# Loading and converting the first three weight pieces ahead of the loop, in a one-core kernel of attention and two MoE layers

## The chip, the cores and the metric

The kernel runs on one core of a Trainium2 chip. The metric is the device time of one execution in microseconds (us), lower is better; three runs of the kernel before are given by their median.

## What is computed

The reference, cut to what matters: an attention that keeps the 32 largest scores of each row, a dense gated MLP ("the first MoE") and a mixture of eight experts with one expert a token ("the second MoE").

```python
# q, k, v: 4 x 8 heads x 576 x 64
scores = scale * np.matmul(q, k.transpose(0, 1, 3, 2))
kth = np.partition(scores, -32, axis=-1)[..., -32:-31]
scores = np.where(scores >= kth, scores, -1e9)
attn = np.exp(scores - scores.max(-1, keepdims=True))
attn = attn / (attn.sum(-1, keepdims=True) + 1e-9)
x = np.matmul(attn, v)                    # 2304 tokens x 512
# first MoE: w_in 512 x 2048, w_out 2048 x 512
h = x @ w_in
x = (h * np.clip(h + 3.0, 0.0, 6.0) / 6.0) @ w_out
# second MoE: 8 experts, 512 -> 1024 -> 512
logits = x @ w_gate
e = argmax(logits); out = softmax(logits)[e] * (relu(x @ w1[e]) @ w2[e])
```

The inputs to the first MoE's weights arrive in 64-bit words, which is why its weights need a conversion.

## The kernel before

**Tiles and stages.** The work of the attention is cut into 144 tiles of 128 query rows of one head (or two heads' tails). Heads go in pairs; a *visit* is a pair of heads with up to 256 of its query rows, four tiles as a rule. Tiles 0 to 3 belong to the first pair, 4 to 7 to the second, and so on. For a pair the kernel loads the keys (tiles `kd` for 512 of them, `ke` for the tail of 64), splits them on POOL (for the first pair on ACT and DVE) into a high and a low part (`kprep`, L434 on), transposes them on PE into `misc` (one buffer, L449 and L457) and copies them to `kx` on ACT (L452, L462). Queries follow in `qprep` (L468 on): loaded to `qn`, transposed (L474), copied to a high part `qh` on ACT (L482), the low part `ql` made on DVE (L492).

For a tile, `qk` writes scores to PSUM (`sps`, four matmuls of L630, two for each half of the keys), `sevac` copies them to an SBUF tile `sbuf` on ACT (L300), `top_a` searches them on DVE: eight MAX8 of 72 columns each (L660, `cd`) and rounds of MAX8 and MATCH_REPLACE (L666, L671, `m` and `cw`). ACT scales the maximum and a threshold (`nb`, `uall`), takes the exponential (L712) and counts signs (L721). For the first 20 tiles a z step finds the exact threshold: POOL writes a mask z (L703, 2.2 us), PE adds it to the scores in `yps` (six matmuls of L630, the first with `identb` as weights; `z_pe`), DVE searches the sum (L731) and masks the exponentials (L735, L739). Then PE transposes them and multiplies with the values (L755, L789).

**The weights of the first MoE.** `conv64` (L309 on) converts one piece of 128 x 512 elements, alternately of `w_in` (i0, i1, ...) and `w_out` (o0, o1, ...), 32 pieces in all. It is a generator with a load step and four more: the load of 512 KB into a `raw` buffer (L316, three buffers); on ACT a square (L328, into `sq`, which is the only buffer of the tag `jk` that also serves the signs of the tiles) and a sign with a sum (L333), on DVE a shift (L329); two more DVE steps (L336, L339); on POOL the copy of the high part (L298) and the subtraction that makes the low one (L347). `conv_load` keeps three pieces loading, `conv_next` takes the front one through its steps and loads another. The loop over tiles takes one piece in nearly every step, `cacc` adding `CRATE` = 15 sixteenths of one. MoE step g forces the pieces that it needs.

**What sets the order.** The program is written tile by tile; a scheduler then orders the instructions of each engine by a priority (`pr`, from a table `PRIO`, lowest first, plus `STEP` = 400 for each step) and its own estimates. After that each engine works strictly in its order, and so does each queue of loads; nearly all loads go through that of the SyncE (SP). A priority can have a lower bound, its second argument. A write of one element into a tile by POOL ahead of its load (L315, from `ts[0]["s"]`, the scores of tile 0) holds the first three piece loads back: they can't start until POOL has read that tile.

The head of the loop before, in which `ensure(t)` prepares the keys and queries that tile t needs:

```python
        loads(0)
        boot.extend([yps[0], yps[1], None, l1ps])
        for t in range(LA):
            ensure(t)
            qk(t)
            sevac(t)
            if t == 0:
                conv_load()
```

Of the kernel before, what the change touches and what calls it, by code (L numbers as in the profile page):

```python
# [13 lines left out]
F32 = mybir.dt.float32  # L14
# [36 lines left out]
    load=-1940, epi_a=370, top_c=55, exp=-295, need=75, qk=10, pv=-40, sevac=390, xevac=440, trans=210, xt0=75,  # L51
# [6 lines left out]
def attention_two_moe_kernel(  # L58
# [13 lines left out]
    PE, V, A, G, SP = nc.tensor, nc.vector, nc.scalar, nc.gpsimd, nc.sync  # L72
# [75 lines left out]
    def r_(ap):  # L148
        return ap.bitcast(F32)
# [4 lines left out]
    def pr(name, least=0):  # L154
        tc.cur_priority = max(least, pr0[0] + PRIO[name])

    def run(gen):
        for _ in gen:
            pass
# [68 lines left out]
    def body(cs, exact, ends=None):  # L228
# [67 lines left out]
        def copy(pool, dst, src):  # L296
            if pool:
                G.tensor_scalar(dst, src, 1.0, 0.0, op0=ALU.mult, op1=ALU.add)  # L298
            else:
                A.activation(dst, src, AF.Copy)  # L300
# [3 lines left out]


        csum = m1p.tile([P, 2 * NF1], F32, name="csum")
        wcnt = [0]

        def conv64(src, a_, nm, parts):  # L309
            n_ = DM // a_  # L310
            pr("load", pbase + 8 * len(wload))
            raw = m1p.tile([P, a_, n_, 2], U32, tag="ysb", bufs=NRAW, name=f"raw{nm}")
            if nm in ("i0", "o0", "i1"):

                G.tensor_copy(raw.rearrange("p a n t -> p (a n t)").bitcast(F32)[:, 0:1], ts[0]["s"][:, 0:1])  # L315
            SP.dma_start(raw.rearrange("p a n t -> p a (n t)"), src)  # L316
            yield
            lo, hi = raw[:, :, :, 0], raw[:, :, :, 1]
            wf = m1p.tile([P, DM], F32, tag="cvs", bufs=3, name=f"cv{nm}").rearrange("p (a n) -> p a n", a=a_)
            wb = wf.bitcast(U32)  # L320
            hf = hi.bitcast(F32)
            sq = ap1.tile([P, S], F32 if exact else BF16, tag="z" if exact else "jk", bufs=2 if exact else 1,
                          name=f"sq{nm}")[:, 0:DM].rearrange("p (a n) -> p a n", a=a_)
            pr("conv")
            if CSQ:
                G.tensor_tensor(sq, hf, hf, op=ALU.mult)
            else:
                A.activation(sq, hf, AF.Square)  # L328
            V.tensor_scalar(wb, hi, 3, 0x3FFFFFFF, op0=ALU.logical_shift_left, op1=ALU.bitwise_and)  # L329
            if not exact:  # L330
                i = wcnt[0]
                wcnt[0] += 1
                A.activation(sq, sq, AF.Sign, bias=cs["ntiny"], scale=1.0, accum_out=csum[:, i:i + 1])  # L333
            yield
            pr("conv")
            V.scalar_tensor_tensor(wb, hi, 0xC0000000, wb, op0=ALU.bitwise_and, op1=ALU.bitwise_or)  # L336
            yield
            pr("conv")
            V.scalar_tensor_tensor(wb, lo, 29, wb, op0=ALU.logical_shift_right, op1=ALU.bitwise_or)  # L339
            if exact:  # L340
                G.tensor_scalar(sq, sq, TINY2, None, op0=ALU.is_ge)
                G.tensor_tensor(wf, sq, wf, op=ALU.mult)
            yield
            pr("conv")
            h, l, done = parts()
            copy(CH, h, wf)
            G.tensor_tensor(l, wf, r_(h), op=ALU.subtract)  # L347
            done()
# [15 lines left out]
        wload = []  # L364

        def conv_load():
            while wsteps and len(wload) < NRAW:
                wload.append(wsteps.pop(0))
                next(wload[-1])
# [4 lines left out]
        def conv_next():  # L374
            if wload:
                yield from wload[0]
                wload.pop(0)
                cdone[0] += 1
                conv_load()
                if not exact and cdone[0] == 2 * NF1:  # L380
                    V.tensor_scalar(csum, csum, DM - 0.5, 0.0, op0=ALU.is_lt, op1=ALU.add, accum_out=flag[:, 1:2])

        def conv_upto(i):
            while cdone[0] <= i:
                run(conv_next())
# [32 lines left out]
        kraw = {}  # L418
# [172 lines left out]
        def ensure(t):  # L591
            n = tiles[t][0]
            b, p = visits[n][:2]
            while kdone[0] <= b * NPAIR + p or qdone[0] <= n:
                loads(t)
                pk[0] = "need"
                pstart(t - 1, -2 * T)
                while pjob[0] is not None:
                    pnext()
                pk[0] = "prep"  # L600
                loads(t)

        ts = {}

        def qk(t, zw=None):
            pr("qk" if zw is None else "zpe")
            n, o = tiles[t]
            b, p = visits[n][:2]
            st = qx[n]
            kt = kx[b, p]  # L610
            for half in range(2):
                dst = (sps if zw is None else yps2)[:, half, 0:HS]
                if o == "T":

                    fw = visits[n][3] // P * P
                    mm = []
                    for i in st:
                        mm.append((dst, i[:, 0, fw:fw + P], kt[0][:, half * HS:(half + 1) * HS]))
                        a_, b_ = half * HS, min((half + 1) * HS, N4)
                        mm.append((dst[:, 0:b_ - a_], i[:, 1, fw:fw + P], kt[1][:, TAIL + a_:TAIL + b_]))  # L620
                        if half:
                            mm.append((dst[:, b_ - a_:HS], i[:, 1, fw:fw + P], kt[1][:, 0:TAIL]))
                else:
                    h, j = o
                    js = slice(j * P, (j + 1) * P)
                    mm = [(dst, i[:, h, js], kt[h][:, half * HS:(half + 1) * HS]) for i in st]
                if zw is not None:
                    mm.insert(0, (dst, identb[0], zw[:, half * HS:(half + 1) * HS]))
                for i, (d_, a_, b_) in enumerate(mm):
                    PE.matmul(d_, a_, b_, start=(i == 0), stop=(i == len(mm) - 1))  # L630

        def sevac(t):
            pr("sevac")
            ssb = sbuf[t % NSB]
            copy(mod(t, SPOOL), ssb.rearrange("p (h s) -> p h s", h=2), sps[:, :, 0:HS])
            ts[t] = {"s": ssb}
# [455 lines left out]
        pbase = pr0[0] = tc.cur_priority + STEP  # L1092
        loads(0)
        boot.extend([yps[0], yps[1], None, l1ps])
        for t in range(LA):
            ensure(t)
            qk(t)
            sevac(t)
            if t == 0:
                conv_load()  # L1100
        cacc = 0
        for t in range(T + 7):
            pr0[0] = pbase + t * STEP
# [317 lines left out]
    with tc.If(todo > 0):  # L1421
# [4 lines left out]
        for e in range(NE):  # L1426
            n = nc.values_load(ctl[0:1, 2 + e:3 + e], min_val=0, max_val=NT)
# [32 lines left out]
```

## Time and profile before

| | |
|---|---|
| median of three runs | 1199.83 us |
| lowest and highest | 1197.64 and 1202.85 us |
| the profiled execution: time | 1204.39 us |
| its span, first to last instruction | 1202.5 us |
| PE busy | 1118.5 us, 93% of the span |
| DVE busy | 940.9 us, 78% |
| ACT busy | 807.6 us, 67% |
| POOL busy | 458.5 us, 38% |
| mean granted clock of PE | 0.961 of full speed |

All times of the trace belong to the one profiled execution and count from its first instruction. A share of busy time is a mean over stages with different bounds: the attention with the first MoE runs to about 930 us, the second MoE after that, and within the attention the start, the stretch with the weight conversion (33 to about 242 us) and the rest differ. An engine's idle time says what ended it; it costs something only where that engine sets the pace.

### The profile page before, as it was taken

The page shows a single profiled execution, that of the slowest core. Times are in us where ns is not written, and L with a number is a line of the kernel's source. Part 1 is how long each engine was busy: PE and PEld are TensorE (multiplying, and loading weights), DVE is VectorE, ACT ScalarE, POOL GpSimd, SP SyncE. Part 2 cuts the span into 40 slices and gives each one's busy share as a digit, 9 for nine tenths or more (in the row PEclk, how much of TensorE's full clock was granted, in tenths as well). Part 3 has the DMA queues.
Part 4 walks back from the last instruction along what each step waited for, and adds up shares of the span by engine and source line. Part 5 has one row for each costly group of instructions (what it writes and reads, how often), then busy time and mean ns, then how long its engine had stood idle before and what let it go on. Part 6 is the DMA issues. An engine that isn't in the chain of part 4 may idle for free.

```text
span 1202.5 us, 24061 instructions
## 1 busy us (share of the span) xinstructions
PE 1118.5 (93%) x7414; PEld 1003.8 (83%) x7414; DVE 940.9 (78%) x3853; ACT 807.6 (67%) x2082; POOL 458.5 (38%) x668
## 2 busy tenths in 40 slices
PE   5677688999999999999999999999999899999995
PEld 4566577778999989999988899999888799888885
DVE  5989989999999999998999899999641554545540
ACT  4777877778878788778778788777541353444441
POOL 5877646644332354433342432322344311222110
PEclk9668879999999999999999999999999899999998
DMA  3654456564553555754444554543486555455530
GB/s 76 189 179 142 143 171 221 162 174 125 157 134 113 151 134 142 177 135 135 118 122 126 133 147 125 152 133 110 127 271 163 176 187 179 161 176 185 160 121 31
DMA packets 184123, 179.24 MB, mean 149 GB/s; under 512 B 123629, under 2 KB 148509, under 8 KB 183984
## 3 DMA queue, kind: packets, MB, share of 16 engines
q1 hardware_dynamic: 178960, 167.24, 48.3%
q0 software_dynamic: 3872, 10.08, 2.6%
q8 instruction: 61, 1.00, 0.4%
q14 instruction: 78, 0.64, 0.2%
q10 hardware_dynamic: 1152, 0.28, 0.1%
HBM read 159.53 MB, written 18.61 MB: 148 GB/s over the span
## 4 chain that ended last, share of the span: by engine, by line
PE 71%; DVE 16%; issue 5%; ACT 4%; POOL 2%; DMA 2%; SPq 0%; POOLq 0%; ACTq 0%; DVEq 0%
PE l1ps L863 15%; PE yps L894 13%; PE ptps L789 9%; PE lp L1263 8%; PE ops L1286 8%; PE sps L630 6%; PE ptps L755 4%; DVE cd L660 2%; DVE pbuf L739 2%; DVE z L696 2%; DVE z L731 1%; PE ptps L935 1%; DVE m L666 1%; DVE cw L671 1%; PE misc L474 1%
## 5 line engine op out<-in xcount | busy, mean ns | idle before, releaser
L894 PE MATMUL yps<-wo,gh 128*128 128x512 f32 x544 | 206.7, 418 | 0.1
L298 POOL TENSOR_SCALAR gh<-gf 128x256 fp32r<-128x256 f32 x144 | 72.7, 505 | 345.2 <-PE yps L894 196.0
L660 DVE MAX8 cd<-sbuf 128x8 f32<-128x72 f32 x1152 | 187.9, 218 | 3.4 <-ACT sbuf L300 3.2
L863 PE MATMUL l1ps<-xh,wih 128*128 128x256 f32 x576 | 167.6, 291 | 4.7 <-DVE gf L875 3.1
L863 PE MATMUL l1ps<-xh,wil 128*128 128x256 f32 x576 | 164.0, 285 | 0.0
L863 PE MATMUL l1ps<-xl,wih 128*128 128x256 f32 x576 | 163.9, 285 | 0.0
L789 PE MATMUL ptps<-vn,pt 128*128 128x65 f32 (+1 forms) x1152 | 145.8, 281 | 0.0
L789 PEld LDWEIGHTS ptps<-vn,pt 128*128 128x128 f32 x1152 | 143.0, 201 | 0.0
L739 DVE SCALAR_TENSOR_TENSOR pbuf<-sbuf,tall,pbuf 128x576 f32<-128x576 f32 x144 | 136.8, 950 | 0.1
L883 POOL TENSOR_TENSOR gl<-gf,gh 128x256 fp32r<-128x256 f32 x144 | 125.5, 871 | 11.4
L863 PEld LDWEIGHTS l1ps<-xh,wih 128*128 128x128 f32 x576 | 110.4, 192 | 14.9 <-DVE gf L875 7.6
L1036 DVE TENSOR_TENSOR wl<-raw,wh 128x1024 fp32r<-128x1024 f32 x64 | 78.6, 1236 | 53.7 <-ACT wh L1035 51.6
L721 ACT ACTIVATE jk<-sbuf,uall 128x576 bf16<-128x576 f32 x144 | 111.6, 775 | 4.2 <-DVE j L735 0.9
L863 PEld LDWEIGHTS l1ps<-xl,wih 128*128 128x128 f32 x576 | 110.6, 192 | 4.2
L712 ACT ACTIVATE pbuf<-sbuf,nb 128x576 f32<-128x576 f32 x144 | 111.2, 775 | 4.1 <-PE ptps L757 0.9
L894 PEld LDWEIGHTS yps<-wo,gh 128*128 128x128 f32 x544 | 101.2, 190 | 14.8 <-POOL qh L486 0.3
L300 ACT ACTIVATE sbuf<-sps 128x576 f32<-128x576 f32 x144 | 92.9, 645 | 30.4 <-PE sps L630 16.5
L869 ACT ACTIVATE gf<-l1ps,three 128x256 f32<-128x256 f32 x144 | 67.9, 471 | 66.9 <-PE l1ps L863 55.7
L755 PE MATMUL ptps<-ident,pbuf 128*128 128x128 f32 x576 | 93.9, 286 | 19.7 <-DVE j L735 12.6
L894 PE MATMUL yps<-wo,gl 128*128 128x512 f32 x272 | 110.4, 406 | 0.6 <-POOL gl L883 0.6
L863 PEld LDWEIGHTS l1ps<-xh,wil 128*128 128x128 f32 x576 | 110.6, 192 | 0.1
L630 PE MATMUL sps<-kx,qh 128*128 128x288 f32 (+2 forms) x336 | 96.8, 319 | 14.3 <-ACT sbuf L300 10.5
(259 smaller groups left out, 2974.7 us busy)
## 6 DMA issues: line engine op xcount, KB each, us to landing
wo<-wod SPq DMA_DIRECT2D x144, 512.0 KB, 3.8
raw<-in_moe_w_dram SPq DMA_DIRECT2D x64, 512.0 KB, 4.3
vn<-in_v_dram SPq DMA_DIRECT2D x96, 128.0 KB, 2.7
rawi<-in_moe_w_in_dram SPq DMA_DIRECT2D x16, 512.0 KB, 4.0
rawo<-in_moe_w_out_dram SPq DMA_DIRECT2D x16, 512.0 KB, 4.6
wod<-wc SPq DMA_DIRECT2D x16, 512.0 KB, 5.6
qn<-in_q_dram SPq DMA_DIRECT2D x126, 64.0 KB, 2.5
yd<-y SPq DMA_DIRECT2D x18, 258.0 KB, 5.1
```

The lines of the kernel that those rows point to most:

```text
L630: PE.matmul(d_, a_, b_, start=(i == 0), stop=(i == len(mm) - 1))
L660: V.max(cd[:, c, :], s[:, c * CK:(c + 1) * CK])
L712: A.activation(d["p"], d["s"], AF.Exp, bias=d["nb"], scale=SCALE)
L721: A.activation(jk, d["s"][:, 0:S], AF.Sign, bias=ts[t]["u"], scale=-1.0, accum_out=d["sg"])
L739: V.scalar_tensor_tensor(d["p"], d["s"], tall[:, t:t + 1], d["p"], op0=ALU.is_ge, op1=ALU.mult)
L755: PE.transpose(ptps[:, c * P:(c + 1) * P], pb[:, c0 + c * P:c0 + (c + 1) * P], ident)
L789: PE.matmul(d_, a_, b_, start=(i == 0), stop=(i == len(mm) - 1))
L863: PE.matmul(dst, a[:, c, fs], b_[:, c, :], start=(n == 0), stop=(n == 3 * NCC - 1))
L883: G.tensor_tensor(gl, gf, r_(gh), op=ALU.subtract)
L894: PE.matmul(acc(bk, tt), a[:, tsl], b_, start=(f == 0 and m == 0), stop=(f == NF1 - 1 and m == 2))
L1263: PE.matmul(lp, a[:, c, fs], b_[:, c, 0:w], start=(n == 0), stop=(n == 3 * NCC - 1))
L1286: PE.matmul(ops_[j][0:n], a, b_[:, ns], start=(f == 0 and i == 0), stop=(f == NF2 - 1 and i == len(ms) - 1))
```

## The change

The first three raw pieces (i0, o0, i1) are asked for ahead of the two leading tiles, their release reads an element of the first pair's loaded keys, the lower bound of their load priority is dropped, and the first two pieces are converted ahead of the loop over tiles. The conversion steps of the three take the priority `match` (560) in place of `conv` (295), and their `cv` and `sq` tiles get a release of their own, two one-element writes by POOL from the scores of tile 0 (i0, o0) or tile 1 (i1).

```diff
-        wcnt = [0]
+        wcnt = [0, 0]
...
-            pr("load", pbase + 8 * len(wload))
+            pr("load", pbase + 8 * len(wload) if wcnt[1] >= 3 else 0); wcnt[1] += 1
             raw = m1p.tile([P, a_, n_, 2], U32, tag="ysb", bufs=NRAW, name=f"raw{nm}")
             if nm in ("i0", "o0", "i1"):

-                G.tensor_copy(raw.rearrange("p a n t -> p (a n t)").bitcast(F32)[:, 0:1], ts[0]["s"][:, 0:1])
+                G.tensor_copy(raw.rearrange("p a n t -> p (a n t)").bitcast(F32)[:, 0:1], r_(kraw[0, 0][0][:, 0, 1, 1, 0:1]))
             SP.dma_start(raw.rearrange("p a n t -> p a (n t)"), src)
             yield
...
-            pr("conv")
+            early = nm in ("i0", "o0", "i1")
+            ck = "match" if early else "conv"
+            pr(ck)
+            if early:
+                G.tensor_copy(wf.rearrange("p a n -> p (a n)")[:, 0:1], ts[nm == "i1"]["s"][:, 0:1])
+                G.tensor_copy(sq.rearrange("p a n -> p (a n)")[:, 0:1], ts[nm == "i1"]["s"][:, 0:1])
...
             yield
-            pr("conv")
+            pr(ck)
             V.scalar_tensor_tensor(wb, hi, 0xC0000000, wb, op0=ALU.bitwise_and, op1=ALU.bitwise_or)
             yield
-            pr("conv")
+            pr(ck)
             V.scalar_tensor_tensor(wb, lo, 29, wb, op0=ALU.logical_shift_right, op1=ALU.bitwise_or)
...
         boot.extend([yps[0], yps[1], None, l1ps])
+        conv_load()
         for t in range(LA):
             ensure(t)
             qk(t)
             sevac(t)
-            if t == 0:
-                conv_load()
+        conv_upto(1)
```

Lines of the changed program behind L324 are numbered five higher than before (L328 is now L333, L492 is L497).

**The order on POOL at its start.** Before, the identity and the iotas follow at once; `jp` and `iota` are index tables, `ident` the identity that all transposes need:

```order
L184 IOTA jp 128x128
masks.py:199 AFFINE_SELECT ident<-ident 128x128
L189 IOTA iota_96 128x8
L192 IOTA isum 128x16
L195 IOTA tok 128x18
```

Now:

```order
L184 IOTA jp 128x128
L315 COPY rawi_187<-kd_0_176 128x1
L315 COPY rawo_190<-kd_0_176 128x1
L315 COPY rawi_193<-kd_0_176 128x1
masks.py:199 AFFINE_SELECT ident<-ident 128x128
L189 IOTA iota_96 128x8
```

The three release copies, which wait for a key load, have moved ahead of the identity and the index tables. They also stand ahead of the key split.

**The order on POOL between tile 1's scores and tile 1's z.** `vp` is a value tile, `sbuf_156` and `sbuf_157` are the scores of tiles 0 and 1, `kd_1` the second pair's keys. Before:

```order
L546 COPY vp_164<-sbuf_157 64x1 x2
L442 TENSOR_SCALAR kd_1_208<-kd_1_208 128x8x64
L443 TENSOR_TENSOR kd_1_208<-kd_1_208 128x8x64
L703 TENSOR_SCALAR z_347<-sbuf_156,uall 128x576
L703 TENSOR_SCALAR z_430<-sbuf_157,uall 128x576
L703 TENSOR_SCALAR z_498<-sbuf_158,uall 128x576
```

Now:

```order
L298 TENSOR_SCALAR wih<-cvi_246 128x4x128
L352 TENSOR_TENSOR wil<-cvi_246,wih 128x4x128
L708 TENSOR_SCALAR z_377<-sbuf_156,uall 128x576
L447 TENSOR_SCALAR kd_1_217<-kd_1_217 128x8x64
L448 TENSOR_TENSOR kd_1_217<-kd_1_217 128x8x64
L298 TENSOR_SCALAR wc_268<-cvo_259 128x512
L352 TENSOR_TENSOR wc_268<-cvo_259,wc_268 128x512
L329 CAST sqi_358<-sbuf_157 128x1
L298 TENSOR_SCALAR wih<-cvi_357 128x4x128
L447 TENSOR_SCALAR ke_1_218<-ke_1_218 64x2x64
L352 TENSOR_TENSOR wil<-cvi_357,wih 128x4x128
L448 TENSOR_TENSOR ke_1_218<-ke_1_218 64x2x64
```

Behind the last row comes tile 1's z. The six conversion instructions of the three pieces have come between, and the split of the second pair's key tail, which used to stand ahead of tile 0's scores.

**The order on PE at the second pair's queries.** `z_430` and `z_460` are tile 1's z, `misc_361` and `misc_391` receive the transposed queries. Before:

```order
L457 MATMUL misc_343<-ident,ke_1_209 128x64 x2
L630 LDWEIGHTS identb
L630 MATMUL yps<-z_430,identb 128x288
L630 MATMUL yps<-kx_0_1_188,qh_218 128x288
L630 MATMUL yps<-kx_0_1_188,ql_219 128x288
L474 MATMUL misc_361<-ident,qn_222 128x128 x4
L630 MATMUL sps<-kx_1_0_265,qh_366 128x288
```

Now:

```order
L462 MATMUL misc_373<-ident,ke_1_218 128x64 x2
L635 LDWEIGHTS identb
L635 MATMUL yps<-z_460,identb 128x288
L635 MATMUL yps<-kx_0_1_197,qh_227 128x288
L635 MATMUL yps<-kx_0_1_197,ql_228 128x288
L635 LDWEIGHTS identb
L635 MATMUL yps<-z_460,identb 128x288
L635 MATMUL yps<-kx_0_1_197,qh_227 128x288
L479 MATMUL misc_391<-ident,qn_231 128x128
L635 MATMUL yps<-kx_0_1_197,ql_228 128x288
L479 MATMUL misc_391<-ident,qn_231 128x128 x3
```

In both orders the queries stand behind tile 1's z; what has moved is that all six z matmuls now follow the key tail, and that the scores of tile 4 come after them with nothing between.

On DVE the second pair's `ql` stands after all of tile 3's search and its first round before; now it stands behind the fourth of tile 3's eight MAX8.

## Rows read from the trace of the kernel before

**Rows 1.** Stretches: length, then busy us (instructions) of PE, PEld, DVE, ACT, POOL.

```profile
12.80:33.45 20.65, 15.88 (x64) 12.37 (x64) 14.84 (x86) 12.44 (x32) 14.13 (x19) 0.92 0.47 123
33.45:60.00 26.55, 15.03 (x73) 12.95 (x72) 26.55 (x68) 20.68 (x51) 23.35 (x22) 0.68 0.64 174
60.00:180.00 120.00, 91.93 (x509) 79.60 (x509) 110.30 (x448) 94.42 (x248) 76.37 (x62) 0.77 0.52 159
...
300.00:400.00 100.00, 99.33 (x736) 92.39 (x736) 96.31 (x452) 81.24 (x230) 29.98 (x53) 1.00 0.49 136
```

**Rows 2.** Waits of DVE, 10 to 35 us; columns: total us, times, longest.

```profile
DVE z L731 <- PE yps L630: 3.9, 2, 2.9
DVE ql L492 <- ACT qh L482: 2.8, 2, 2.6
DVE cd L660 <- ACT sbuf L300: 2.5, 2, 1.9
```

**Rows 3.** Timeline, 4 to 15 us; columns: start, duration, engine, line, operation.

```profile
4.33 1.28 ACT L439 ACT_TABLE_LOAD   x1 [4.33 <-DMA kd<-in_k_dram]
...
6.28 0.69 DVE L440 TENSOR_TENSOR kd<-kd 128x512 fp32r<-128x512 f32 x1 [5.14 <-ACT kd L439]
...
7.83 0.15 DVE L210 SCALAR_TENSOR_TENSOR place<-lead,own 24x8 f32<-24x8 f32 x1
...
12.80 0.65 ACT L300 ACTIVATE sbuf<-sps 128x576 f32<-128x576 f32 x1 [0.35 <-PE sps L630]
...
13.49 1.18 DVE L660 MAX8 cd<-sbuf 128x8 f32<-128x72 f32 x8 [1.86 <-ACT sbuf L300]
```

**Rows 4.** Single lines over the span; durations in ns are min/median/max.

```profile
L329 DVE TENSOR_SCALAR cvi<-rawi x16: 400/406/1450, 33.5 to 231.2; 128x512 uint32<-128x512 uint32 x16
...
L336 DVE SCALAR_TENSOR_TENSOR cvi<-rawi,cvi x16: 665/670/678, 34.4 to 231.7; 128x512 uint32<-128x512 uint32 x16
...
L339 DVE SCALAR_TENSOR_TENSOR cvi<-rawi,cvi x16: 671/678/994, 35.2 to 232.5; 128x512 uint32<-128x512 uint32 x16
...
L347 POOL TENSOR_TENSOR wil<-cvi,wih x16: 1272/1281/1918, 38.7 to 234.1; 128x512 fp32r<-128x512 f32 x16
...
L739 DVE SCALAR_TENSOR_TENSOR pbuf<-sbuf,tall,pbuf x144: 792/810/1924, 23.5 to 863.3; 128x576 f32<-128x576 f32 x144
...
L315 POOL COPY rawi<-sbuf x2: 188/190/192, 14.1 to 14.4; 128x1 f32<-128x1 f32 x2
```

**Rows 5.** A load on the queue of SP, and loads from 0 to 60 us.

```profile
13.14 0.62 SPq L528 DMA_DIRECT2D qn<-in_q_dram  x1
...
rawi<-in_moe_w_in_dram SPq DMA_DIRECT2D x5, 512.0 KB, 4.1
```

**Rows 6.** 33.45 to 60 us: busy DVE, POOL of cvi; of cvo; two timeline rows.

```profile
33.45:60.00 26.55, 8.36 (x10) 7.14 (x6) 0.68 0.64 174
...
33.45:60.00 26.55, 8.45 (x9) 5.82 (x6) 0.68 0.64 174
...
38.67 1.57 POOL L347 TENSOR_TENSOR wil<-cvi,wih 128x512 fp32r<-128x512 f32 x1
...
39.05 1.81 DVE L739 SCALAR_TENSOR_TENSOR pbuf<-sbuf,tall,pbuf 128x576 f32<-128x576 f32 x1
```

**Rows 7.** POOL in the timeline, 16 to 23 us, and z matmuls in the chain.

```profile
16.21 0.62 POOL L442 TENSOR_SCALAR kd<-kd 128x512 fp32r<-128x512 f32 x1
...
20.81 2.21 POOL L703 TENSOR_SCALAR z<-sbuf,uall 128x576 bf16<-128x576 f32 x1 [0.30 <-ACT uall L684]
...
20.56 1.64 PE yps L630 x6
```

**Rows 8.** Timeline of the second pair's queries.

```profile
25.03 1.11 PE L474 MATMUL misc<-ident,qn 128*128 128x128 f32 x4
...
26.18 0.60 ACT L482 ACTIVATE qh<-misc 128x512 fp32r<-128x512 f32 x1 [0.94 <-PE misc L474]
...
26.81 0.69 DVE L492 TENSOR_TENSOR ql<-misc,qh 128x512 fp32r<-128x512 f32 x1 [0.21 <-ACT qh L482]
```

## The prediction

> **What bounds the kernel now.** I read the busy time by stretches first, then VectorE's (DVE's) waits in the start, then the timeline of the first 31 us. The stretches [rows 1] show the start as the one loose place: from 12.80 to 33.45 us, when the first tiles are searched, DVE works 14.84 of 20.65 us, so 5.81 are free. From 33.45 to 60 it works 26.55 of 26.55, from 60 to 180 110.30 of 120: while weights are converted, DVE sets the pace. From 300 to 400 TensorE (PE) works 99.33 of 100; there PE does. So time saved or lost on DVE in the first 40 us moves what lies behind it by about as much, while idle time of PE, ScalarE (ACT) or GpSimd (POOL) in the start costs nothing by itself.
>
> DVE's waits between 10 and 35 us [rows 2] are z of the first tiles behind PE (3.9 us in two waits, the longer 2.9), ql behind ACT (2.8 in two, the longer 2.6) and the search behind ACT's score copies (2.5 in two, the longer 1.9). The longer ql wait and the longer search wait lie before 13.49, where the search begins [rows 3].
>
> **The change, part by part.** *The three pieces.* One piece costs DVE 0.406 + 0.670 + 0.678 = 1.75 us by the medians of L329, L336 and L339 [rows 4], three of them 5.26. POOL pays 1.28 for the low half and about 0.62 for the high one (as for the key's high half, a tile of the same size) [rows 4, 7], 1.90. They leave the stretch behind 33.45 and go between the searches of tiles 0 to 2. On DVE 5.26 would fit into the 5.81 free ones. That is the whole direct gain, if nothing new is made to wait.
>
> *The release.* The three POOL copies now read a key element and wait for the keys' load, which had landed when ACT began at 4.33 [rows 3]. By the order of POOL the identity and the iotas stand behind them. At 0.19 us each [rows 4] they end by 4.9; they used to be done with long before. So DVE's small constants, which end about 7.8 as before [rows 3], now have eight of their instructions ahead of the key split: it goes from 6.28 to about 7.5, 1.2 us late. Against that, ACT now copies tile 0's scores before the second head's keys: split to 8.2, four transposes 1.1, key copy 0.6 [rows 8], four score matmuls 1.1 (six z matmuls take 1.64 [rows 7]) and the gaps between them; tile 0's copy can begin at about 11.5, where it was 12.80 [rows 3]. Tile 1 has a piece's two activations ahead of it on ACT and gains less. I take nothing for the start, with bounds -1.3 and +1.2.
>
> *The queue of SP.* The second pair's last query part went out at 13.14 [rows 5]. Two of the three piece loads and a value load, which waits for tile 1's scores, now stand ahead of it; it goes at about 16.5. A piece lands 4.1 us after its issue, also with other loads about [rows 5]. So the queries are there by about 20 and the third piece by about 18, and what wants the queries comes later still (next part). POOL's queue is the cover; were it short, the second pair would wait at 20 us for these loads.
>
> *The new wait.* This term decides. Between tile 1's score copy and tile 1's z, POOL had the key split and two z, from 16.21 on [rows 7]. Now the order of POOL gives it three conversions (3 x 1.90), two z (2 x 2.21), the key split (0.62 and, as for L347, 1.28), the key tail's (about 0.7, by its size a third of that) and a small cast (0.2): 12.9 us. From about 16.0 tile 1's z ends at 28.9, against 20.81 + 2.21 = 23.02. PE holds the second pair's query transposes behind that z: six z matmuls, 1.64, then the transposes to 31.1, qh 0.60 to 31.7, ql 0.69 to 32.4. Before, ql ended at 27.50 [rows 8]. And ql stands in the midst of tile 3's search, so DVE stops there.
>
> *DVE's account to that point.* Before, from 13.49 to 27.50, 14.01 us with 2.9 + 0.2 of waiting [rows 2, 3, 8]: 10.9 of work. Now 1.55 of it (tile 1's z search, four search steps and one round) stands behind ql: 9.35, plus 5.26 makes 14.6, from about 12.2. DVE would be through at 26.8 and is let through at 32.4. Made equal, 32.4 + 1.55 = 33.95 against 27.50 + 5.26 = 32.76: **1.2 us late**, with the pieces done.
>
> *What follows.* Before, two more waits came behind ql, 3.9 - 2.9 = 1.0 (z) and 2.5 - 1.9 = 0.6 (tile 5) [rows 2]. DVE now gets to both places late, and I leave 0.5 for tile 5: credit 1.1. Two things I can only bound. From 33.45 to 60 the 19 conversion instructions take 8.36 + 8.45 = 16.81 us [rows 6] where the medians make 10.9, a surcharge of 0.93 a piece. Three pieces fewer there save between 0, as the next ones crowd in, and 2.8. And the third pair's ql also stands behind POOL's queue: 0 to 2.3 of new waiting (tile 5's copy plus the activations ahead of that ql on ACT, less the search in between). I set the two against each other.
>
> *Contention.* L739 takes 0.810 by its median and 1.81 where it began 0.38 us after a POOL subtract [rows 4, 6]. The Trainium skill (GPSIMD Engine Reference, section 8, Key points) says that GpSimd shares its SBUF interfaces with VectorE and contends with VectorE instructions that run in a 2-port mode or have two SBUF inputs; the rows agree. By that rule the pieces would carry their surcharge, 2.8 us in all, into the start, where z and the splits keep POOL busy: it speaks against the change, and the sum would come to +2.9. By the rows most of the surcharge would fall into DVE's wait at ql, and I count none.
>
> **Sum:** 0 (start) + 1.2 - 1.1 + 0 = +0.1. The profiled execution took 1204.39 us, so 1204.5 in its frame; it lies 4.56 above the median of the runs, 1199.83. That gives 1199.9, and I say **1200.0**. The other 29 pieces come one a tile as before, on a DVE that is still the bound, so that conversion is two pieces ahead from then on gains nothing that is not in this account.
>
> **The rivals.** *Faster: the pieces lie in idle time.* If POOL's queue does not reach the second pair, for instance because the splits come sooner than I stack them, all 5.26 is hidden and some of the 2.8 goes too: -5.3 to -8.0, about 1193.5. For it: 5.81 us free. Against it: PE's order, which fixes the queries behind tile 1's z. Chance 0.17.
>
> *Slower: POOL becomes the bound of the first three pairs.* Every z passes through POOL at 2.2, behind what was queued. It decides once POOL is so far behind that DVE also stops at the z of tiles 2 and 3 and at the third pair's ql. DVE had no free time from 33.45 to 60; if it gets as much there as in the stretch ahead, 5.81, with the 1.2 of the start it is +7.0, 1206.8. For it: POOL worked 23.35 of 26.55 there already. Against it: the conversions that it did there are gone. Chance 0.13.
>
> *The change doesn't do what it says.* The copies read the element as loaded, not as split, and a piece may come late: the third is issued behind a key load that waits for PE. Price at most 1 us near 18, inside the wait at ql: 1200 again, in the forecast's chance of 0.70.
>
> **How the numbers follow.** Half a per cent, 6 us, is what a measurement of this kernel can tell from no change; its three runs spread over 5.2. The forecast lies within it: faster 0.17, same 0.70, slower 0.13. Its own range is -1.3 - 2.8 = -4.1 to +1.2 + 2.3 = +3.5, with 2 for the runs 1194 to 1205.5. To leave out no more than 2 in 10 the range goes to 1193 and 1207.
>
> **What would show it.** Right: the identity on POOL after 4.7; tile 0's copy before 12; tile 1's z ending between 27 and 30; DVE waiting 2 us or more at ql near 30; the last conversion earlier by some us, and the second MoE within 4 us of where it begins now. Wrong: ql before 28 with the pieces done (faster), or DVE idle by more than 3 us between 34 and 60 (slower). If the start is as I say and the end still moves by more than 5 us, the cause lies in a later place that I have not read.

## The result: 1.0% slower, and the profile after

The changed kernel takes 1211.80 us (median of 4 runs, 1210.13 to 1214.18), the kernel before beside it 1199.14 (4 runs): a ratio of 1.0102, 95% interval 1.008 to 1.0125. The forecast was 1200.0, no change. The profiled execution of the changed kernel took 1210.61 us, with a span of 1208.7. Lines of the changed kernel's file behind line 324 are 5 higher than before: L329 is L334, L492 is L497, L703 is L708, L739 is L744.

**The start came as forecast.** Timeline of the changed kernel (start, duration, engine, line, operation, idle time before), rows that answer to [rows 3, 5]:

```profile
4.00 0.29 POOL masks.py:199 TENSOR_SCALAR_AFFINE_SELECT ident<-ident 128x128 f32<-128x128 f32 x1
7.23 0.69 DVE L445 TENSOR_TENSOR kd<-kd 128x512 fp32r<-128x512 f32 x1
11.55 0.65 ACT L300 ACTIVATE sbuf<-sps 128x576 f32<-128x576 f32 x1 [1.30 <-PE sps L635]
12.23 0.91 DVE L665 MAX8 cd<-sbuf 128x8 f32<-128x72 f32 x6 [2.23 <-ACT sbuf L300]
16.35 0.62 SPq L533 DMA_DIRECT2D qn<-in_q_dram  x1
```

The search begins at 12.23 us, 1.3 earlier than before (13.49), and the last part of the second pair's queries is issued at 16.35, where I had about 16.5.

**Then VectorE stops twice.** Its waits from 10 to 60 us, to be held against [rows 2] (total us, times, longest; the shorter of the two ql waits, 0.98 us, is that of the first pair at 9.31):

```profile
DVE ql L497 <- ACT qh L487: 8.0, 2, 7.1
DVE z L736 <- PE yps L635: 3.4, 1, 3.4
DVE cd L665 <- ACT sbuf L300: 2.2, 1, 2.2
DVE cvi L334 <- DMA rawi<-in_moe_w_in_dram: 1.0, 1, 1.0
DVE j L740 <- ACT jk L726: 1.0, 1, 1.0
```

The stretches that answer to [rows 1] (length, then busy us and instructions of PE, PEld, DVE, ACT, POOL):

```profile
12.23:33.45 21.22, 10.87 (x39) 7.95 (x38) 14.76 (x62) 11.64 (x29) 15.92 (x24) 1.00 0.40 105
33.45:60.00 26.55, 14.61 (x70) 11.74 (x70) 20.42 (x67) 17.52 (x43) 20.99 (x20) 0.81 0.51 151
```

Two stretches tell it. Up to 33.45 VectorE does no more work than before (14.76 against 14.84 us), although three pieces were put there: it stands at ql instead of searching. From 33.45 to 60 it worked without a gap before (26.55 of 26.55) and now 20.42.

What it waits for is GpSimd's queue, and then ScalarE's and TensorE's. Timeline of the changed kernel, GpSimd from tile 1's scores to the third pair's keys, and the rows of the other engines that belong to it:

```profile
16.30 0.61 POOL L298 TENSOR_SCALAR wih<-cvi 128x512 fp32r<-128x512 f32 x1
17.00 1.47 POOL L352 TENSOR_TENSOR wil<-cvi,wih 128x512 fp32r<-128x512 f32 x1
18.57 2.28 POOL L708 TENSOR_SCALAR z<-sbuf,uall 128x576 bf16<-128x576 f32 x1
20.93 0.97 POOL L447 TENSOR_SCALAR kd<-kd 128x512 fp32r<-128x512 f32 x1
21.99 1.57 POOL L448 TENSOR_TENSOR kd<-kd 128x512 fp32r<-128x512 f32 x1
...
25.44 0.72 POOL L329 CAST sqi<-sbuf 128x1 bf16<-128x1 f32 x1
...
28.75 2.22 POOL L708 TENSOR_SCALAR z<-sbuf,uall 128x576 bf16<-128x576 f32 x1
33.54 0.60 ACT L487 ACTIVATE qh<-misc 128x512 fp32r<-128x512 f32 x1 [2.96 <-PE misc L479]
34.03 0.77 ACT L717 ACTIVATE pbuf<-sbuf,nb 128x576 f32<-128x576 f32 x1
34.16 0.69 DVE L497 TENSOR_TENSOR ql<-misc,qh 128x512 fp32r<-128x512 f32 x1 [7.05 <-ACT qh L487]
34.70 0.19 ACT L689 ACTIVATE uall<-m 128x1 f32<-128x1 f32 x1
34.98 2.21 POOL L708 TENSOR_SCALAR z<-sbuf,uall 128x576 bf16<-128x576 f32 x1 [4.01 <-ACT uall L689]
37.98 1.26 POOL L448 TENSOR_TENSOR kd<-kd 128x512 fp32r<-128x512 f32 x1
39.30 1.12 PE L454 MATMUL misc<-ident,kd 128*128 128x128 f32 x4 [1.48 <-POOL kd L448]
40.46 0.46 PE L635 MATMUL yps<-z,identb 128*128 128x288 bf16 x1
42.19 0.77 DVE L736 MAX8 z<-yps 128x8 f32<-128x576 f32 x1 [3.38 <-PE yps L635]
```

The first stop: tile 1's z begins at 28.75, with the three conversions, the key splits and tile 0's z ahead of it without a gap; behind its matmuls stand the second pair's query transposes, then qh at 33.54, then ql. The second stop follows from the first: tile 2's threshold u (L689) stands on ScalarE behind qh and the exponential, so it comes at 34.70, and GpSimd, by then idle for 4.01 us, begins tile 2's z at 34.98. Its matmuls on TensorE (40.46) stand behind the transposes of the third pair's keys (39.30), whose split GpSimd makes after that z. VectorE gets that z at 42.19. This place on TensorE is new: before, tile 2's z stood ahead of those transposes.

```profile
27.66 0.28 PE L630 MATMUL yps<-z,identb 128*128 128x288 bf16 x1 [0.43 <-POOL z L703]
29.72 1.12 PE L449 MATMUL misc<-ident,kd 128*128 128x128 f32 x4 [0.72 <-POOL kd L443]
```

In the changed kernel the z was written by 37.19, and VectorE was through with its search at 38.80. Had the six z matmuls (1.64 us [rows 7]) begun at 37.82, when TensorE had ended what it did before those transposes, they would have ended near 39.5: by this estimate a stop of 0.7 us instead of 3.38. No run changes that order alone.

**How much of the 12 us this is.** The delay is read from the start of the mask instruction (L739, now L744) of a tile, in the mean of two profiles of each kernel (the second ones are runs of the next section):

```
tile                        0      3      9     15     60    141
before, us               23.3   51.5   90.6  125.9  400.6  855.2
changed, later by us      1.3    8.3    8.4    8.0    7.8    5.8
```

All of it is there by tile 3, 60 us into the run, and behind tile 60 some 2 us of it go again. The two profiles of before are of executions near the top of its runs (1204.39 and 1206.39). Each run lists its mean granted TensorE clock: 11 executions of before at 0.960 to 0.961 have a mean span of 1201.9 us, the five of the changed kernel, with a mean clock of 0.9604, one of 1210.1. At equal clock that is 8.2 us, the delay of tile 3. All 63 executions of before that ran beside the experiments have a mean clock of 0.9645 and a mean span of 1199.7: another 2.2 us, which go with a lower clock of the changed kernel. About 2 us of the difference between the first medians are left.

### The profile page after: what moved, and what is told of

The parts are those of the page before. It is cut to its first block, busy times and chain, and to the rows that moved or that the text cites. A ratio compares the mean times of both kernels' runs of the same rounds, so it can differ in the third digit from the quotient of the medians.

```text
span 1208.7 us, 24061 instructions
## 1 busy us (share of the span) xinstructions
PE 1119.1 (93%) x7414; PEld 1005.2 (83%) x7414; DVE 943.5 (78%) x3853; ACT 807.3 (67%) x2082; POOL 454.3 (38%) x674
## 4 chain that ended last, share of the span: by engine, by line
PE 66%; DVE 17%; issue 5%; ACT 5%; DMA 3%; POOL 2%; SPq 0%; POOLq 0%; ACTq 0%; DVEq 0%
PE l1ps L868 13%; PE yps L899 11%; PE ptps L794 9%; PE lp L1268 8%; PE ops L1291 8%; PE sps L635 5%; PE ptps L760 4%; DVE cd L665 3%; DVE pbuf L744 2%; DVE z L701 2%; DVE z L736 2%; DVE m L671 1%; DVE cw L676 1%; PE ptps L940 1%; PE sps L899 1%
## 5 line engine op out<-in xcount | busy, mean ns | idle before, releaser
L744 DVE SCALAR_TENSOR_TENSOR pbuf<-sbuf,tall,pbuf 128x576 f32<-128x576 f32 x144 | 143.0, 993 | 0.1
L888 POOL TENSOR_TENSOR gl<-gf,gh 128x256 fp32r<-128x256 f32 x144 | 121.8, 846 | 11.4
L701 DVE SCALAR_TENSOR_TENSOR z<-sbuf,uall 128x576 f32<-128x576 f32 x124 | 106.8, 862 | 0.0
```

Of the source, the lines that this page charges most:

```text
L701: V.scalar_tensor_tensor(d["z"], s, d["u"], s, op0=ALU.is_le, op1=ALU.mult)
L744: V.scalar_tensor_tensor(d["p"], d["s"], tall[:, t:t + 1], d["p"], op0=ALU.is_ge, op1=ALU.mult)
L888: G.tensor_tensor(gl, gf, r_(gh), op=ALU.subtract)
```

## The experiments

Theories: **queue** (GpSimd's added work ahead of what the second and third pair need delays VectorE), **loads** (the early piece loads hold up the second pair's on the queue of SyncE), **ScalarE** (its order and added activations do), **later place** (the cost arises behind the first 60 us).

**1. The conversions behind tile 1's z.** The six GpSimd instructions are put back in the program until tile 1's threshold is there, and a one-element copy from it makes them wait:

```
+            def fin(dep=None):
...
+                h, l, done = parts()
+                if dep is not None:
+                    G.tensor_copy(h[:, 0:1, 0:1].rearrange("p a n -> p (a n)"), dep)
+                copy(CH, h, wf)
+                G.tensor_tensor(l, wf, r_(h), op=ALU.subtract)
+                done()
+            held.append(fin) if early else fin()
...
+            if t == 2:
+                while held:
+                    held.pop(0)(ts[t - 1]["m8"][:, 0:1] if exact else uall[:, t - 1:t])
```

> The changed kernel with one thing undone: the six GpSimd instructions of the three early pieces wait for tile 1's threshold and stand behind tile 1's z. Loads, VectorE's order and ScalarE's work stay those of the change. Queue theory (the GpSimd work ahead of tile 1's z made the second pair's queries late): tile 1's z ends near 24 us instead of 31.0, the first ql of the second pair runs before 29 us with under 1.5 us of idle time ahead of it instead of 7.05, and the time falls from 1211.8 to 1197-1203. Theory that the early loads get in the way on the queue of SyncE, or that ScalarE's extra activations do: ql stays near 34 and the time within 3 us of 1211.8. Theory of a later place (the starts differ by some 6 us, the medians by 12.7): the idle time goes, but the time stops at 1204-1207.

Measured: 1211.79 us, 1.0087 (1.0065 to 1.0108): a miss for the queue theory as I had put it. Timeline of that kernel:

```profile
24.62 2.21 POOL L714 TENSOR_SCALAR z<-sbuf,uall 128x576 bf16<-128x576 f32 x1 [1.86 <-ACT uall L695]
28.05 0.47 PE L468 MATMUL misc<-ident,ke 64*128 64x64 f32 x2 [2.46 <-POOL ke L454]
31.62 0.69 DVE L503 TENSOR_TENSOR ql<-misc,qh 128x512 fp32r<-128x512 f32 x1 [6.09 <-ACT qh L493]
33.54 2.21 POOL L714 TENSOR_SCALAR z<-sbuf,uall 128x576 bf16<-128x576 f32 x1
40.73 0.77 DVE L742 MAX8 z<-yps 128x8 f32<-128x576 f32 x1 [4.30 <-PE yps L641]
```

Tile 1's z is 4 us earlier than in the change, yet ql waits 6.09: TensorE first takes the transposes of the key tail, whose split now stands among the dependence copies behind z. And the three conversions now stand ahead of tile 2's z, which begins at 33.54 (25.40 before), and VectorE stops there for 4.30. The stops add up to 10.4 us, as in the change (7.05 + 3.38). GpSimd's work was moved, not taken away.

**2. The early loads alone.** One line out:

```
-        conv_upto(1)
```

> The changed kernel without the conversion of two pieces ahead of the loop over the tiles: three pieces are released and loaded as early as in the change, and converted one a tile as before, so that one conversion (1.9 us of GpSimd) stands ahead of tile 1's z instead of three. Queue theory: z of tile 1 is 1 to 2 us later than before, time 1199-1203. Theory of the loads: the second pair's queries land late as in the change, ql waits by more than 4 us, time 1207-1212.

Measured: 1200.92 us, 0.9991 (0.9981 to 1.0002), no difference from before.

```profile
22.55 2.22 POOL L708 TENSOR_SCALAR z<-sbuf,uall 128x576 bf16<-128x576 f32 x1
29.50 0.69 DVE L497 TENSOR_TENSOR ql<-misc,qh 128x512 fp32r<-128x512 f32 x1 [1.68 <-ACT qh L487]
```

The loads theory falls: same release, same queue of SyncE, and ql waits 1.68 us at most. In its profile the masks come 1.7 us earlier than before at tile 3 and 4.2 at tile 60, of which the timed runs show 1.5 us in the medians at most; that execution had a mean granted clock of 0.969, those of before 0.961 and 0.960.

**3. GpSimd's work alone, in the kernel before.**

```
+            if t == 1:
...
+                sc = ts[1]["s"][:, 0:DM].rearrange("p (a n) -> p a n", a=NCC)
+                for i_ in range(3):
+                    sl_ = slice(i_ * P, (i_ + 1) * P)
+                    G.tensor_scalar(wih[:, :, sl_], sc, 1.0, 0.0, op0=ALU.mult, op1=ALU.add)
+                    G.tensor_tensor(wil[:, :, sl_], sc, r_(wih[:, :, sl_]), op=ALU.subtract)
```

> The kernel before with three pairs of GpSimd instructions added, of the shapes of the three conversions (copy and subtract, 128 partitions by 512), reading tile 1's scores and placed ahead of the z of tiles 0 and 1; their results are overwritten later. Nothing else is changed: the loads and VectorE's and ScalarE's work are those of before. Queue theory: tile 1's z ends near 28-29 us, VectorE stops at ql for 4 us or more, and the time rises from 1199 by 5 to 8 us, to 1204-1207. Theories of the loads or of ScalarE: the time stays within 2 us of before.

Measured: 1209.43 us, 1.0066 (1.0048 to 1.0084), 7.0 us above the 1202.41 of before measured beside it.

```profile
22.32 2.22 POOL L703 TENSOR_SCALAR z<-sbuf,uall 128x576 bf16<-128x576 f32 x1
26.25 0.77 DVE L731 MAX8 z<-yps 128x8 f32<-128x576 f32 x1 [6.11 <-PE yps L630]
```

So 5.7 us of GpSimd work, with nothing else of the change, cost 7.0. VectorE stops for 6.11 us at tile 0's z instead of at ql, since five of the six instructions stand ahead of it here (the last subtract comes between the z of tiles 0 and 1). The forecast of the place was wrong; the rise of 5 to 8 us was right, though not the 1204 to 1207 that it was worked out to, since before ran at 1202.41 beside it.

**4. The kernel before again.** No edit.

> The kernel before, unchanged, for a second profile: the first one was of an execution 5 us above the median. Expected near 1199, and a span that is shorter than the first profile's in the later stages rather than in the first 60 us; if the first 60 us differ, the comparison of the two starts has to be made against this one.

One execution, 1206.39 us, span 1204.5, and not near 1199 as expected. Its masks run 1.2 us ahead of the first profile up to tile 15 and 1.2 behind from tile 70 on; between 420 and 430 us the granted clock was 0.83. The starts agree, and the comparison stands.

**5. One piece ahead of the loop instead of two.**

```
-        conv_upto(1)
+        conv_upto(0)
```

> The changed kernel with one piece converted ahead of the loop instead of two: in GpSimd's order two conversions (3.8 us) instead of three stand ahead of tile 1's z, and the second pair's key tail stands behind that z. Queue theory: tile 1's z ends 2 to 4 us earlier than in the change (27-29 us instead of 31.0), VectorE waits 3-5 us at ql instead of 7.05, and the time lies between that of the loads-only run (1200.9) and that of the change (1211.8), at 1203-1208. Theory that the chain has a step at the second piece alone: 1200-1202 or 1210-1212.

Measured: 1208.81 us, 1.0068 (1.0042 to 1.0094), 0.8 us above the range that was expected.

```profile
25.03 2.60 POOL L708 TENSOR_SCALAR z<-sbuf,uall 128x576 bf16<-128x576 f32 x1
32.09 0.69 DVE L497 TENSOR_TENSOR ql<-misc,qh 128x512 fp32r<-128x512 f32 x1 [4.59 <-ACT qh L487]
39.32 0.77 DVE L736 MAX8 z<-yps 128x8 f32<-128x576 f32 x1 [2.72 <-PE yps L635]
```

The dose is in the row of ql: with one, two and three conversions ahead of tile 1's z (run 2, this run, the change) it waits 1.68, 4.59 and 7.05 us. At tile 2's z VectorE does not wait in run 2, 2.72 us here and 3.38 in the change. Runs 2 and 5 have the same order on TensorE at the queries (tile 1's z, the key tail, the queries): tile 1's z ends at 24.77 and 27.63 us on GpSimd, and ql begins at 29.50 and 32.09. So with TensorE's order the same, GpSimd's later z makes the queries later by nearly as much.

Both profiles have a mean granted clock of 0.969 and can be held against each other: the masks of run 5 are 4.2 us later than those of run 2 at tile 3, 6.0 at tile 9 and 8.5 at tile 141. Half of this run's loss arises behind tile 3, other than in the change; at what place is not shown.

**6. GpSimd relieved.**

```
-            copy(CH, h, wf)
-            G.tensor_tensor(l, wf, r_(h), op=ALU.subtract)
+            if early:
+                A.activation(h, wf, AF.Copy)
+                V.tensor_tensor(l, wf, r_(h), op=ALU.subtract)
```

> The changed kernel with the three early pieces' high halves made by ScalarE and their low halves by VectorE; GpSimd has none of the three conversions. Loads and the places of the pieces stay those of the change, VectorE has three subtracts more (some 2 us). Queue theory (it is the time that GpSimd works ahead of tile 1's z, whatever is in its way on ScalarE): ql comes before 29 us, VectorE waits under 2 us there, time 1195-1202. Theory that ScalarE's order is the cause (tile 1's and tile 2's thresholds behind key copies and qh): ScalarE has more to do here, so the wait stays over 4 us and the time at 1208 or more.

Measured: 1201.53 us, 1.0015 (0.9993 to 1.0037). ScalarE has more to do, VectorE three subtracts more, and the loss is gone. VectorE's waits from 10 to 60 us hold neither ql nor a z of over 0.4 us:

```profile
DVE cvo L334 <- DMA rawo<-in_moe_w_out_dram: 2.9, 2, 1.9
...
DVE z L740 <- PE yps L639: 0.4, 1, 0.4
```

In this kernel the scheduler also put the query transposes ahead of tile 1's z on TensorE, so it does not tell GpSimd's share from that of TensorE's order; runs 2 and 5 do, and run 3 adds GpSimd's work alone.

**7. Thresholds u of tiles 1 and 2 earlier on ScalarE.**

```
                 d["u"] = uall[:, t:t + 1]
+                if t in (1, 2):
+                    tc.cur_priority = max(0, tc.cur_priority - 2 * STEP)
```

> The changed kernel with the thresholds u of tiles 1 and 2 put earlier on ScalarE: tile 1's ahead of the second pair's first key copy, tile 2's ahead of qh. By GpSimd's order tile 1's z then also stands ahead of the third conversion. Work is the same. If the second stop (z of tile 2, 3.38 us, behind the threshold that stood behind qh) is a cost by itself, it goes: GpSimd's idle 4.0 us ahead of tile 2's z vanishes, VectorE waits under 1 us at tile 2's z, and the time falls by 3-6 us to 1206-1209. If VectorE would only wait elsewhere (queue theory in its strict form: GpSimd's sum of work up to the third pair's keys sets the pace), the time stays at 1210-1213.

Measured: 1210.54 us, 1.0077 (1.0056 to 1.0098).

```profile
32.94 0.77 DVE L738 MAX8 z<-yps 128x8 f32<-128x576 f32 x1 [5.27 <-PE yps L635]
...
38.60 0.23 DVE L665 MAX8 cd<-sbuf 128x8 f32<-128x72 f32 x1 [2.09 <-ACT sbuf L300]
```

The stop at tile 2's z is gone (its matmuls now follow the z at once, at 35.53, ahead of the third pair's transposes), and VectorE stops elsewhere: 5.27 us at tile 1's z, 2.09 at the search of tile 4. The loss is 10.5 us against the 12.7 of the change, with intervals that overlap: what a better place for ScalarE's small instruction is worth, if anything, can't be told.

**8. Both: conversions behind tile 1's z, and u earlier.** The edits of 1 and 7 together, and the preparation of the second pair's keys earlier as well, which the expectation does not name:

```
+            if (b, p) == (0, 1):
+                tc.cur_priority = max(0, pbase - 2 * STEP)
```

> The run with the three conversions behind tile 1's z, and with the thresholds u of tiles 1 and 2 earlier on ScalarE as well. In the first of these runs tile 1's z still waited 1.86 us for its threshold, which stood behind the second pair's key copy, and the matmuls of that z stood behind the transposes of the key tail. Expected if both the queue and ScalarE's order count: z of tile 1 ends near 25, ql before 30 us, time 1200-1206. If GpSimd's total work up to 38 us decides, wherever it stands: VectorE waits for the z of tile 2 instead, and the time stays at 1209-1212.

Measured: 1207.91 us, 1.0062 (1.0046 to 1.0079), between the two expectations.

```profile
34.64 0.40 PE L643 MATMUL yps<-z,identb 128*128 128x288 bf16 x1 [3.65 <-POOL z L718]
37.70 0.23 DVE L673 MAX8 cd<-sbuf 128x8 f32<-128x72 f32 x1 [5.00 <-ACT sbuf L300]
```

The stop at ql shrinks to 0.59 us, with 2.61 at tile 1's z ahead of it, but TensorE now has tile 2's z in the midst of tile 4's score matmuls and waits 3.65 us for GpSimd, and the search of tile 4 stands for 5.00 behind those scores.

**9. Two tries at something better.** Run 6 with the edit of 7; and the early loads of run 2 with the edits of 6 and 7.

> The run with GpSimd relieved of the three conversions, with the thresholds u of tiles 1 and 2 earlier on ScalarE as well (there tile 1's z still began at 26.9 us, after 2.6 us of idle time of GpSimd behind that threshold). If what ScalarE's order costs comes on top of the queue: z of tile 1 begins near 23-24, no wait of VectorE over 1 us from 20 to 40 us, time 1 to 3 us below the 1201.5 of that run. If VectorE was never late there for it: 1200-1203, no difference.

> The early loads, with no piece converted ahead of the loop (one a tile, as before), the first three pieces' halves made by ScalarE and VectorE in place of GpSimd, and the thresholds u of tiles 1 and 2 earlier on ScalarE. In TensorE's order the z of tile 1 stands ahead of the second pair's query transposes, as in the change. Queue theory: with GpSimd free that order does no harm, VectorE waits under 2 us at ql, time 1194-1200, the shortest of all kernels here. Theory that TensorE's order alone makes the queries late: VectorE waits 4 us or more at ql, time above 1203.

Measured: 1205.13 us, 1.0024 (1.0004 to 1.0044), and 1204.95 us, 1.0025 (1.0012 to 1.0037): neither beats before, and both expectations of a gain were missed. The second one was meant to settle the order on TensorE: there tile 1's z stands ahead of the query transposes as in the change. VectorE has no wait at ql between 20 and 40 us, but only because it stands for 2.25 us just ahead of it:

```profile
30.77 0.60 ACT L491 ACTIVATE qh<-misc 128x512 fp32r<-128x512 f32 x1
30.78 0.69 DVE L353 TENSOR_TENSOR wc<-cvo,wc 128x512 fp32r<-128x512 f32 x1 [2.25 <-ACT wc L352]
31.40 0.69 DVE L501 TENSOR_TENSOR ql<-misc,qh 128x512 fp32r<-128x512 f32 x1
```

VectorE's own subtract waits for ScalarE's copy, and qh is done at 31.37, 4.6 us later than before (26.78 [rows 8]); ql could not have begun sooner. So the queries are late here with GpSimd free of the three conversions, and the time lies where the theory of TensorE's order had it (above 1203). What that order, or ScalarE's, costs by itself stays open.

**10. The changed kernel again.** No edit.

> The changed kernel, unchanged, for a second profile. Expected: the same two stops of VectorE (7 us at ql near 34, 3.4 us at the z of tile 2 near 42), 1208-1214 us; the stretches behind 60 us may differ with the granted clock by some us.

One execution, 1211.69 us, and the same two stops, ql 7.05 and tile 2's z 3.38.

**What they say together.** A count made after the runs: take the conversions that GpSimd makes ahead of tile 2's z or of the third pair's key split. Where it is three, the time is 0.6 to 1.0% above before, wherever among those they stand (runs 1, 3, 5, 7, 8 and the change); where it is two, none or they are on other engines, within 0.3% (runs 2, 6 and 9; in run 2, the only one with two, the third stands behind the third pair's keys, at 34.91 us). Before, GpSimd had little room there. Its timeline, tile 2's z:

```profile
25.40 2.21 POOL L703 TENSOR_SCALAR z<-sbuf,uall 128x576 bf16<-128x576 f32 x1 [2.38 <-ACT uall L684]
```

From 16.21 us to this z it idled 2.38 us here and 0.30 ahead of tile 1's z [rows 7], 2.7 in all, and the change asks for 5.7. The loads and ScalarE's added activations are in runs 2 and 6 too and cost nothing there that can be told. For the change the later place falls as well: nearly all of the delay is there by tile 3; for run 5 it does not. Nor is a free GpSimd enough: the second kernel of run 9 has a mean clock of 0.969 and a mean span of 1202.8 us, where ten executions of before at 0.968 to 0.970 have 1197.0, so at equal clock it loses 5.8 us to other waits. Shown are that GpSimd's work alone costs 7.0 us (run 3) and that ql waits by its dose (runs 2 and 5); how the rest divides between the orders of TensorE and ScalarE, which the scheduler changed in nearly every run, is not. No version was faster than before beyond its interval; run 2 is the nearest.

## Why the prediction was wrong

*The start*: right. Split 7.23 (forecast about 7.5), tile 0's copy 11.55 (11.5). The identity came at 4.00, where the sign was "after 4.7": the release copies were done sooner than I had put.

*The queue of SP*: right, and confirmed by run 2: the second pair's queries did not wait for it.

*GpSimd's chain to tile 1's z*: the place and the mechanism were right, the size 2.1 us short. It was to end at 28.9, by its sign between 27 and 30, and ended at 30.97. The key split took 0.97 + 1.57 us where I had 0.62 + 1.28, the cast 0.72 where I had 0.2, the first subtract 1.47 where I had 1.28; the rest are six gaps of 0.08 to 0.10 us between instructions, which I had not counted, and a start at 16.30. The longer ones ran beside long instructions of VectorE, of the pieces or a mask.

*The wait at ql*: VectorE was to arrive at 26.8 and be let through at 32.4; it arrived at 27.11 and ql ended at 34.85. From the z's end to the last query transpose the working took 2.2 us, where its own rows make 2.75 (1.64 + 1.11); 2.5 were measured. By that account the pieces were done 3.6 us late (34.85 + 1.55 against 32.76) instead of 1.2.

*What follows*: **this step failed, and it is the larger part of the miss.** The sum took 4.8 us off the time behind ql: 5.26 for the three pieces that were no longer to be done there and a credit of 1.1, because DVE would reach the z of tile 2 and the copy of tile 5 late, less 1.55 of search. Nothing came off. From the end of ql to tile 3's mask, before and in the changed kernel (length, then busy us of PE, PEld, DVE, ACT, POOL):

```profile
27.50:52.13 24.63, 13.05 (x68) 11.02 (x68) 22.89 (x64) 18.25 (x43) 20.14 (x21) 0.75 0.59 166
34.85:59.75 24.90, 13.70 (x66) 11.21 (x67) 19.48 (x66) 15.96 (x41) 20.74 (x20) 0.81 0.53 157
```

VectorE works 3.4 us less there and stands 3.7 us longer, 5.42 us instead of 1.74: 3.38 at tile 2's z, 1.0 at j (L740, the small step ahead of the mask, which waits for ScalarE's signs), 1.0 at the load of a piece. And only one piece fewer is converted in the stretch, four instead of five: by tile 3's mask the changed kernel has done seven pieces, before five. The next pieces crowded in. So the delay at tile 3, 8.3 us in the mean of the profiles, is 7.6 at the end of ql, where the working had 4.9, and 0.7 behind it, where it had a gain of 4.8.

Of the second stop I had followed GpSimd's queue to tile 1's z and left it there. The next item, tile 2's z, needs a threshold that stands on ScalarE behind qh, that is behind the queries that I had just made 5 us late; and on TensorE its matmuls had moved behind the third pair's transposes.

*The rivals*: the slower one, GpSimd as the bound of the first three pairs, is what happened in the main. It named the z of tile 2, and its sign, DVE idle by more than 3 us between 34 and 60, came; there was no stop at tile 3's z or at the third pair's ql. Its price, 7.0 us in the profile's frame, was 1.3 short, and its chance of 0.13 too low. Against it I had held that the conversions that GpSimd did behind 33 us are gone. From 33.45 to 60 us it has five conversion instructions instead of twelve, but VectorE has no use for that while it stands. The faster rival had 5.81 us of free time on its side; but GpSimd, which feeds VectorE there, had only 2.7 us to give, and that was not looked at.

*The contention term*: that the pieces carry a surcharge into the start was right, and that it falls into the wait at ql too. The nine VectorE instructions of the three pieces take 6.86 us where the medians make 5.26, the worst two beside a GpSimd subtract (17.00 to 18.47 us) and tile 0's z (18.57 to 20.85):

```profile
17.40 1.36 DVE L334 TENSOR_SCALAR cvo<-rawo 128x512 uint32<-128x512 uint32 x1
18.87 1.03 DVE L341 SCALAR_TENSOR_TENSOR cvo<-rawo,cvo 128x512 uint32<-128x512 uint32 x1
```

VectorE still came to ql at 27.11. By the rule of the Trainium skill (GPSIMD Engine Reference, section 8) all of the surcharge, which [rows 6] put at 2.8 us, would have come along into the start. 1.6 show, and not on the path. That the longer GpSimd instructions of the chain above have the same reason is likely by the overlap and not shown by a run.

*The frame*: the sum was made against one execution 4.56 us above the median. At equal clock the change costs 8.2 us; against the medians the changed kernel lost 4.5 us more, of which 2.2 go with the lower granted clock. Why that clock is lower was not tested.

## What to carry to other kernels

Free time on the engine that sets the pace is not free if it is waiting time for a second engine whose queue is full: before work is moved into it, read the idle time of the second engine in that stretch too, here 2.7 us for the 5.7 that were added. Follow a late result through every queue it passes, past the first wait that it causes: a small instruction behind it on a third engine (here a threshold of 0.19 us) starts the next stop, and a changed order on a fourth can lengthen it. Work that is moved out of a stretch shortens it only if nothing moves up into its place. And when work on the crowded engine is moved, look at whether the sum of the stops falls or only their places change.

## What the runs showed of the hardware

A stretch of about 10 us in which the loads nearly stop and TensorE's granted clock halves, in some executions only. Stretch 640 to 650 us (length, busy us of PE, PEld, DVE, ACT, POOL, clock, DMA share, GB/s) of run 8 and, of the same stretch, run 1:

```profile
640.00:650.00 10.00, 9.96 (x41) 8.96 (x42) 5.44 (x26) 4.59 (x13) 0.56 (x4) 0.53 0.03 7
```

```profile
640.00:650.00 10.00, 8.77 (x65) 7.75 (x65) 8.63 (x43) 7.51 (x25) 1.68 (x5) 1.00 0.24 82
```

TensorE was busy for 9.96 us there, with clock 0.53, 41 matmuls in place of 65, and across it the masks fall back by 4.7 us against those of run 1 (from 1.7 ahead at tile 102 to 3.0 behind at tile 105). Runs 6 and 7 have it too (0.66 and 0.60 in the stretch of ten us that is lowest); run 5 (290 to 300 us) and the second profile of before (420 to 430) have a lesser one, 0.83 each. The first profile of before and those of the change have none behind 250 us. The 63 executions of before lie between 1196.70 and 1205.70 us, and such a stretch can be a part of that; what sets it off stays open.
